# Where the 128 unread filling steps of a TensorE queue stand, and how wide their products are

## The chip, the cores and the metric

The kernel runs on one core of one Trainium2 chip. The metric is device time in microseconds (us) of one launch, from which the median over several runs is taken. A profiled execution has a time of its own, and inside it a span, from the first to the last instruction that the profiler shows.

## The reference

The computation has two stages. The first is a recurrent attention (RWKV7) over 768 time steps for 4 batches x 8 heads, with a 40x40 state for each of the 32 sequences. The second is a normalised SwiGLU feed-forward network on the 3072 x 320 result.

```python
for t in range(S):                                   # S = 768
    y[:, :, t] = einsum('bhd,bhde->bhe', rt, state)
    Sa = einsum('bhde,bhe->bhd', state, at)
    state = state * wt[:, :, None, :] - einsum('bhd,bhe->bhde', Sa, bt) + einsum('bhd,bhe->bhde', vt, kt)
...
xn = x / sqrt(mean(x * x) + 1e-6) * rms_g            # x: (3072, 320)
g, val = xn @ w_gate, xn @ w_val                     # (320, 1536) each
out = (g * sigmoid(g)) * val @ w_out                 # (1536, 320)
```

The feed-forward weights arrive in 64-bit floating point.

## The kernel before, in words

The 768 time steps are cut into 24 chunks of 32. For each chunk `front(c)` loads the chunk's inputs, turns them (TensorE transposes, line 479) and makes the chunk's triangular matrices level by level (`gramk`, line 476: the steps named A,K and Ab,K). `inverse(c)` sends the triangular matrix through DRAM into another layout (DMA sB, M), inverts it on VectorE (Yi and tmp) and sends it back (DMA sY, LT). `main(c)` solves for the chunk's update (the steps Xs,LT and Xs,LB, used in the first five chunks), updates the state (VU,KN and ST), and makes the chunk's output y (the steps As,KN and As,kbn, one for each level), which is normalised and turned into `xg`. `feed(g)` then runs the feed-forward network for one or two chunks: twelve column blocks with weights `wf`, accumulated into the PSUM tile `po` (line 476, po<-wf,hT). The weights are narrowed from 64 to 32 bits once, in pieces, by `narrow` (lines 988 to 996 and the helpers: tiles `wf`, `exs`, `o`, on VectorE and ScalarE, with loads from GpSimd's queue); this is laid among the first chunks.

No scheduler runs. Each operation is recorded as a `Piece` by `Plan.add`, in the order of the Python code, and `Plan.issue` issues the pieces in the order of the table `ORDER`, written out by hand. A number in `ORDER` counts from the first piece that is not yet issued; 0 is that piece itself. So numbers after a moved piece change even where the order of the other pieces doesn't. Each engine then works through its own queue in that order and waits in it where an input isn't there yet.

The intermediate results of TensorE live in three PSUM tiles, ps0 to ps2. Each use of one is a "room", and the table `PAIRS` says for each room which of the three it gets.

The last 128 pieces are recorded at the end of the kernel function (lines 1024 to 1029) and are of kind "idle". Each issues two bf16 products of 128x128 by 512 columns of the identity's bits into the half `po_[:, 1]` of `po`. Nothing reads what they write; the first product of the network's accumulation overwrites it. They wait for nothing but the identity, and no other engine waits for them. In this text such a piece is a filling step, and its two products are fillers. All of them stand in the first 166 us.

## Time and profile before

| | us |
|---|---|
| runs: median (lowest to highest, 3 runs) | 1004.35 (996.09 to 1010.13) |
| the profiled execution, its own time | 1002.48 |
| its span | 1000.7 |
| TensorE busy in the span | 955.2 |
| VectorE busy | 776.7 |
| ScalarE busy | 507.3 |
| GpSimd busy | 343.4 |
| fillers (line 1028), 256 products, busy | 70.5 |
| TensorE's mean granted clock | 0.994 |

In the profile PE is TensorE, PEld its weight loads, DVE VectorE, ACT ScalarE, POOL GpSimd and SP the queue engine; a q behind a name is the engine's sequencer. A float32 product of one matmul stands as two instructions in the trace, a transpose and a filler as one. The ends of matmuls are modelled, so that the time from start to start says more of their pace than their own length. The granted clock (PEclk in an answer by stretches) is the share of full speed at which TensorE was let run.

### The profile page before, as it was taken

Reading aid. Unit: us, or ns where it says so; the run is one execution under the profiler, and the core shown is the slowest. Engines: PE = TensorE matmul, PEld = TensorE weight load, DVE = VectorE, ACT = ScalarE, POOL = GpSimd, SP = SyncE. Lnnn points to the kernel's source line nnn. Section 1 sums busy time; section 2 is a strip of 40 time slices with the busy share of each in tenths; the row PEclk is TensorE's granted clock in tenths of the full one; section 3 lists DMA queues with packets and bytes.
Section 4 is the critical chain, followed back from the end, with each engine's and each line's share of the span. In section 5 each row is a group of like instructions: output and inputs, shape, how many; then the busy total and the mean of one; then the engine's idle time right before and its main releaser. Section 6 shows DMA issues by size and latency. Waiting matters only on the chain.

```text
span 1000.7 us, 55765 instructions
## 1 busy us (share of the span) xinstructions
PE 955.2 (95%) x24768; PEld 754.0 (75%) x24768; DVE 776.7 (78%) x2721; ACT 507.3 (51%) x1133; POOL 343.4 (34%) x592
## 2 busy tenths in 40 slices
PE   8788799999999999999999999999999899999998
PEld 4455557877877887888888788878787787788877
DVE  9998877786977977977969878879689588676541
ACT  6787467455454444454553554545544445435131
POOL 8887353231242333334132333331504224211000
PEclk9999999999999999999999999999999999999999
DMA  8665343322233323233132332332323232320100
GB/s 176 170 178 134 81 110 76 66 53 51 43 68 69 52 63 76 44 79 77 25 73 40 78 78 41 77 72 37 79 57 59 55 63 60 63 40 17 41 11 20
DMA packets 139025, 68.89 MB, mean 69 GB/s; under 512 B 119617, under 2 KB 126113, under 8 KB 138785
## 3 DMA queue, kind: packets, MB, share of 16 engines
q0 software_dynamic: 19680, 32.48, 15.5%
q1 hardware_dynamic: 116928, 32.53, 14.8%
q8 instruction: 194, 3.18, 1.3%
q10 hardware_dynamic: 2176, 0.33, 0.2%
q14 instruction: 47, 0.38, 0.1%
HBM read 55.05 MB, written 10.22 MB: 65 GB/s over the span
## 4 chain that ended last, share of the span: by engine, by line
PE 71%; DVE 11%; DMA 6%; ACT 4%; issue 4%; POOL 2%; SPq 2%; DVEq 0%; ACTq 0%; POOLq 0%
PE ps L476 51%; PE po L476 13%; PE ps L479 6%; DVE Yi L430 2%; SPq L473 2%; DMA M<-sB 2%; DMA sB<-LT 2%; DMA LT<-sY 1%; PE po L1028 1%; DVE tmp L430 1%; DVE LT L430 1%; DVE As L430 1%; ACT VU L457 1%; DMA sY<-Yi 1%; DVE K L430 1%
## 5 line engine op out<-in xcount | busy, mean ns | idle before, releaser
L476 PE MATMUL ps<-xg,wf 128*128 128x256 f32 (+3 forms) x1872 | 362.4, 375 | 2.6 <-DVE hT L430 2.5
L476 PEld LDWEIGHTS ps<-xg,wf 128*128 128x128 f32 (+1 forms) x1872 | 268.1, 189 | 51.4 <-issue 5.9
L476 PE MATMUL po<-wf,hT 128*128 128x320 f32 x576 | 178.5, 442 | 0.3 <-DVE hT L430 0.3
L476 PEld LDWEIGHTS po<-wf,hT 128*128 128x128 f32 x576 | 104.7, 190 | 34.4 <-DVE hT L430 0.5
L430 DVE TENSOR_TENSOR Yi<-Yi,tmp 128x24 f32<-128x24 f32 (+21 forms) x512 | 107.3, 210 | 11.0
L430 DVE TENSOR_TENSOR tmp<-Yi,M 128x24 f32<-128x24 f32 (+21 forms) x512 | 107.4, 210 | 10.9 <-DMA M<-sB 0.3
L430 DVE TENSOR_TENSOR hT<-ps,sg 128x256 f32<-128x256 f32 (+1 forms) x156 | 60.1, 400 | 71.0 <-PE ps L476 49.0
L453 ACT ACTIVATE sg<-ps 128x256 f32<-128x256 f32 (+1 forms) x156 | 55.0, 369 | 110.7 <-PE ps L476 110.2
L463 POOL TENSOR_TENSOR ss<-ss,mhalf 128x1 f32<-128x1 f32 x24 | 16.9, 704 | 252.2 <-DVE ss L430 237.7
L457 ACT COPY KN<-ps 128x640 f32<-128x640 f32 x95 | 65.7, 693 | 70.0 <-DVE LT L430 29.5
L430 DVE TENSOR_TENSOR K<-K,T 128x256 f32<-128x256 f32 (+1 forms) x191 | 93.7, 502 | 2.9 <-PE ps L476 1.7
L430 DVE SCALAR_TENSOR_TENSOR Yi<-M,Yi 128x27 f32<-128x27 f32 (+7 forms) x228 | 46.2, 243 | 52.6 <-DMA M<-sB 25.3
L473 POOL DMA_DIRECT2D kbn<-in_b_dram x92 | 53.9, 587 | 91.6 <-PE ps L476 90.6
L473 POOL DMA_DIRECT2D kbn<-in_k_dram x92 | 53.8, 587 | 81.7 <-PE ps L476 80.4
L476 PEld LDWEIGHTS ps<-Ab,K 64*60 64x60 f32 (+2 forms) x4608 | 66.1, 127 | 20.4 <-issue 9.0
L473 POOL DMA_DIRECT2D VU<-in_v_dram x92 | 54.0, 588 | 78.8 <-PE ps L476 74.9
L476 PE MATMUL ps<-Ab,K 64*60 64x56 f32 (+2 forms) x4608 | 73.0, 214 | 6.8 <-DVE K L430 2.6
L430 DVE TENSOR_TENSOR As<-ps,msi 128x256 f32<-128x256 f32 (+1 forms) x168 | 70.7, 455 | 7.6 <-ACT As L460 4.9
L476 PEld LDWEIGHTS ps<-As,KN 128*40 128x40 f32 x3072 | 63.9, 124 | 15.2 <-issue 5.5
L1028 PE MATMUL po<-ident 128*128 128x512 bf16 x256 | 70.5, 401 | 2.0 <-POOL ident L492 2.0
L476 PE MATMUL ps<-As,KN 128*40 128x32 f32 x3072 | 68.9, 204 | 3.4 <-ACT y L457 1.3
L457 ACT COPY K<-K 128x512 f32<-128x512 f32 x95 | 60.6, 638 | 19.4 <-DVE K L430 6.9
(141 smaller groups left out, 1554.1 us busy)
## 6 DMA issues: line engine op xcount, KB each, us to landing
M<-sB SPq DMA_DIRECT2D x24, 512.0 KB, 4.4
wan<-in_r_dram SPq DMA_DIRECT2D x24, 160.0 KB, 3.7
kbn<-in_b_dram POOLq DMA_DIRECT2D x92, 40.0 KB, 3.1
VU<-in_v_dram POOLq DMA_DIRECT2D x92, 40.0 KB, 2.6
wan<-in_w_dram POOLq DMA_DIRECT2D x46, 80.0 KB, 2.9
wan<-in_a_dram POOLq DMA_DIRECT2D x46, 80.0 KB, 2.6
kbn<-in_k_dram POOLq DMA_DIRECT2D x92, 40.0 KB, 2.7
wn<-in_w_dram POOLq DMA_DIRECT2D x92, 40.0 KB, 2.8
```

What stands on the lines that cost most here:

```text
L430: plan.add("DVE", time + more + each * size(o), 0.087, lambda at: [fn(at(o), *m(at))], [o], aps(*args))
L453: scalar(o, [a], lambda at: nc.scalar.activation(at(o), at(a), f, **kw), aps(acc), 0.1 if f in (AF.Square, AF.Relu) else 0.0)
L457: scalar(o, [a], lambda at: nc.scalar.copy(at(o), at(a)), extra=more)
L463: plan.add("POOL", 0.5, 0.06, lambda at: nc.gpsimd.tensor_tensor(o, a, b, op), [o], [a, b])
L473: plan.add(by, 0.6 if by == "POOL" else 0.45, 0.0, lambda at: queue.dma_start(out=o, in_=i), [o], [i], load=load, since=since)
L476: return o, lhsT, rhs, lambda at: nc.tensor.matmul(at(o), lhsT, rhs, start=start, stop=stop, skip_group_check=True), 4
L479: return o, i, ident, lambda at: nc.tensor.transpose(at(o), i, ident), 2
L1028: nc.tensor.matmul(po_[:, 1], ones[:, 0:P], ones[:, None, :].to_broadcast((P, 2, 2 * P)), start=True, stop=True, skip_group_check=True)
```

## The change

Two things change. Each filler has 384 columns in place of 512. And the 128 filling steps stand at other places: the order of all other pieces is the same, piece for piece, on all engines, and the number of filling steps is too. From the chunk-0 output's last transposes on (the step ps<-ident,y at 76.30 us in the trace of before), the table `PAIRS` also has ps1 and ps2 exchanged.

```diff
 ORDER = """
 76 84 83 86 75 71 2 3 4 5 6 7 0 35 47 0 17 54 64 0 0 51 0 35 0 55 0 0 67 68 60 187 188 41 49 368 59 71 369 0
-35 0 0 0 46 353 374 182 5903 5904 5905 5906 5907 73 0 32 167 168 178 75 74 73 0 1 27 3 0 362 2 0 346 367 337 170 2 164 163 336 72 80
+35 0 0 0 46 353 374 182 5903 5904 5905 5906 5907 5908 5909 5910 5911 73 0 32 167 168 178 75 74 73 0 1 27 3 0 362 2 0 346 367 337 170 2 164
...
 PAIRS = """
-012020012010102101021011100001020010220212110200010202110021221002100001122012021010121222112121201101021101101102221210
+012020012010102101011012200002020020110121220100020101220012112001200002211021012020212111221212102202012202202201112120
...
     for n in range(IDLE):
         plan.add("PE", 0.0, 0.0, lambda at: [
-            nc.tensor.matmul(po_[:, 1], ones[:, 0:P], ones[:, None, :].to_broadcast((P, 2, 2 * P)), start=True, stop=True, skip_group_check=True)
+            nc.tensor.matmul(po_[:, 1, 0:384], ones[:, 0:P], ones[:, None, 0:192].to_broadcast((P, 2, 192)), start=True, stop=True, skip_group_check=True)
             for k in range(2)], [], [ident], kind="idle", many=4)
```

How many filling steps stand in front of a TensorE step, for the steps where it changes most or where the prediction speaks of it (times are starts in the trace of before):

| step | at us | before | after |
|---|---|---|---|
| ps<-ident,wan (first transposes) | 6.42 | 5 | 9 |
| ps<-A,K (chunk 1) | 30.50 | 6 | 0 |
| ps<-ident,kbn (chunk 2) | 47.82 | 13 | 23 |
| ps<-ident,K (chunk 1) | 51.62 | 4 | 1 |
| ps<-Xs,LB (chunk 0) | 56.59 | 1 | 4 |
| ps<-rE,vut (chunk 0) | 64.10 | 1 | 0 |
| ps<-As,KN and As,kbn (chunk 0, four steps) | 68.99 to 72.15 | 3 | 0 |
| ps<-Xs,LT (chunk 1) | 77.21 | 1 | 0 |
| ps<-Ab,K (chunk 2, last) | 91.62 | 3 | 4 |
| ps<-As,kbn and VU,KN (chunk 1) | 99.36, 101.25 | 1, 1 | 0, 0 |
| ps<-ST,aP (chunk 2) | 109.91 | 1 | 0 |
| ps<-ident,K (chunk 2) | 113.27 | 3 | 0 |
| ps<-Xs,LT (chunk 2, first) | 124.31 | 1 | 7 |
| ps<-Xs,LB (chunk 2) | 126.85 | 4 | 1 |
| ps<-As,kbn (chunk 2) | 141.38 | 1 | 6 |
| ps<-As,KN (chunk 2, third and fourth) | 143.72, 145.90 | 1, 1 | 2, 0 |
| ps<-ident,wan; ident,x; Xs,LT | 148.78, 150.34, 152.80 | 5 | 0 |
| all steps from Xs,LT to ps<-xg,wf | 155.90 to 166.11 | 5 | 0 |

Three places on TensorE. The first is the output of chunk 1, at 98 to 101 us: the level steps with chunk 1's factors KN_1 and kbn_95, and the update VU_99. Before:

```order
L476 MATMUL ps_65<-As_136,KN_1_107 40x32 x16
L1028 LDWEIGHTS ident
L1028 MATMUL po<-ident 128x512
L1028 LDWEIGHTS ident
L1028 MATMUL po<-ident 128x512
L476 MATMUL ps_65<-As_136,kbn_95 40x32 x16
L476 MATMUL ps_63<-As_136,KN_1_113 40x32 x16
```

After, at the same place on TensorE:

```order
L476 MATMUL ps_64<-As_136,KN_1_107 40x32 x16
L476 MATMUL ps_64<-As_136,kbn_95 40x32 x16
L476 MATMUL ps_63<-As_136,KN_1_113 40x32 x16
L476 MATMUL ps_65<-VU_99,KN_1_115 40x40 x32
L476 MATMUL ps_63<-As_136,KN_1_111 40x32 x16
```

The filling step between the two level steps is gone, and so is the one ahead of VU_99; ps_64 and ps_65 (ps1 and ps2) are exchanged.

The second place is TensorE at 25 to 30 us, between chunk 0's VU_98,LT_102 (the first product of its solve) and chunk 1's first A_122,K_121. Before, where eleven more fillers follow the last row:

```order
L1028 LDWEIGHTS ident
L1028 MATMUL po<-ident 128x512
L476 MATMUL ps_65<-VU_98,LT_102 32x40 x32
L1028 LDWEIGHTS ident
L1028 MATMUL po<-ident 128x512
```

After, on TensorE from the transposes of kbn_95 on:

```order
L479 MATMUL ps_65<-ident,kbn_95 104x64 x16
L479 MATMUL ps_63<-ident,K_120 128x40 x16
L479 MATMUL ps_64<-ident,wan_93 104x64 x16
L476 MATMUL ps_65<-VU_98,LT_102 32x40 x32
L476 MATMUL ps_63<-A_122,K_121 64x56 x32
L476 MATMUL ps_64<-Ab_124,K_120 60x56 x32
```

Twelve filling steps that stood between these six rows are gone; the next filler comes behind the last row.

The third place is TensorE at 157 to 163 us, chunk 4's first level steps (A_122,K_120 and Ab,K) and the transposes of chunk 3's VU_99. Before:

```order
L1028 LDWEIGHTS ident
L1028 MATMUL po<-ident 128x512
L476 MATMUL ps_65<-A_122,K_120 64x56 x32
L479 MATMUL ps_64<-ident,VU_99 104x64 x16
L1028 LDWEIGHTS ident
L1028 MATMUL po<-ident 128x512
L1028 LDWEIGHTS ident
L1028 MATMUL po<-ident 128x512
L476 MATMUL ps_63<-Ab_123,K_121 60x56 x32
L476 MATMUL ps_64<-Ab_124,K_120 56x56 x32
```

After, on TensorE:

```order
L476 MATMUL ps_65<-Xs_133,LT_103 32x40 x32
L476 MATMUL ps_64<-A_122,K_120 64x56 x32
L479 MATMUL ps_65<-ident,VU_99 104x64 x16
L476 MATMUL ps_63<-Ab_123,K_121 60x56 x32
L476 MATMUL ps_65<-Ab_124,K_120 56x56 x32
```

No filling step stands here or later; before, the last one stood at 165.68 us.

## The prediction, made before the result was known

> **What bounds the kernel now.** I read the page first, then the fillers alone by stretch, then the chain of waits in the part that holds them, then TensorE in order of time.

> ```profile
> span 1000.7 us, 55765 instructions
> PE 71%; DVE 11%; DMA 6%; ACT 4%; issue 4%; POOL 2%; SPq 2%; DVEq 0%; ACTq 0%; POOLq 0%
> L1028 PE MATMUL po<-ident 128*128 128x512 bf16 x256 | 70.5, 401 | 2.0 <-POOL ident L492 2.0
> ```

> The chain that ended last is 71% TensorE. The fillers are one group of 256 products; the 2.0 us of idle time before them is the start. Now the fillers alone in three stretches (stretch, its length, busy time and count on PE and PEld, granted clock, DMA share, GB/s), and below them, for the first stretch, all engines (PE, PEld, DVE, ACT, POOL).

> ```profile
> 0.00:62.00 62.00, 31.82 (x118) 10.64 (x118) 0.97 0.74 179
> 62.00:170.00 108.00, 38.63 (x138) 10.01 (x138) 0.97 0.46 107
> 170.00:1000.70 830.70, 0.00 (x0) 0.00 (x0) 1.00 0.27 56
> ```

> ```profile
> 0.00:62.00 62.00, 49.35 (x1030) 26.75 (x1030) 57.82 (x187) 45.97 (x83) 52.40 (x103) 0.97 0.74 179
> ```

> After 170 us there is no filler, the clock is full, and nothing in the order changes: 831 us can only be moved as a whole. So the change is worth what it does before 170 us. In the first 62 us VectorE is busy for 57.82 us, with weight narrowing, and the chain has no piece of line 1028; a filler there costs nothing so far. From 62 us on the chain has these (start, length, what; 16 pieces, of which I quote the first, the last and those that the sum uses):

> ```profile
> 63.64 0.54 PE po L1028 x2
> 76.74 0.54 PE po L1028 x2
> 90.13 1.40 PE po L1028 x6
> 98.89 0.54 PE po L1028 x2
> 100.78 0.54 PE po L1028 x2
> 109.44 0.54 PE po L1028 x2
> 111.94 1.40 PE po L1028 x6
> 113.96 0.54 PE po L1028 x2
> 125.09 1.83 PE po L1028 x8
> 145.00 0.97 PE po L1028 x2
> 148.31 0.54 PE po L1028 x2
> 163.09 0.54 PE po L1028 x2
> 165.84 0.43 PE po L1028 x2
> ```

> The three pieces left out are like the one at 163.09 (two products, 0.54 us; at 155.43, 156.69 and 159.34). All sixteen make 12.0 us, the 1.2% that the chain's summary gives to this line. This is time in which a filler ran and the chain's next step stood behind it.

> **Pace of a filler.** TensorE in order of time (start, length, what, count, idle time before and what ended it):

> ```profile
> 2.04 4.45 PE L1028 MATMUL po<-ident 128*128 128x512 bf16 x10 [2.04 <-POOL ident L492]
> 25.57 0.79 PE L476 MATMUL ps<-VU,LT 32*32 32x40 f32 x64
> 30.50 1.16 PE L476 MATMUL ps<-A,K 64*64 64x56 f32 x64 [1.44 <-ACT KN L457]
> 39.39 5.79 PE L1028 MATMUL po<-ident 128*128 128x512 bf16 x26
> 47.82 1.10 PE L479 MATMUL ps<-ident,kbn 64*104 64x64 f32 x16 [2.64 <-POOL kbn L469]
> 56.59 0.79 PE L476 MATMUL ps<-Xs,LB 16*32 16x40 f32 x64 [0.85 <-ACT Xs L457]
> 83.41 1.81 PE L476 MATMUL ps<-A,K 64*64 64x56 f32 x64
> 141.38 0.81 PE L476 MATMUL ps<-As,kbn 128*40 128x32 f32 x32 [1.69 <-ACT x L460]
> 143.72 1.28 PE L476 MATMUL ps<-As,KN 128*40 128x32 f32 x32
> 164.49 1.36 PE L476 MATMUL ps<-xg,wf 64*128 64x128 f32 x12
> ```

> At full clock 26 fillers take 5.79 us, 0.22 each; at the start, before the clock is up, ten take 4.45 us, 0.45 each. By columns (384 of 512) that becomes 0.17 and 0.33, so a filling step of two takes 0.33 us, or 0.67 at the slow clock. All 256 then take 43 us in place of 57. That the pace follows the columns is an assumption, though the slow and the full clock's 2 to 1 speaks for it.

> **Part by part: what leaves the path.** At ten places of 0.54 us on the chain, at 145.00 (0.97) and at 165.84 (0.43) the changed order has no filling step before that step any more: 10 x 0.54 + 0.97 + 0.43 = 6.8 us. At 125.09 four steps become one. The step behind them needs Xs, which ScalarE writes:

> ```profile
> 125.23 0.41 ACT L457 COPY Xs<-ps 128x320 f32<-128x320 f32 x1
> 127.76 0.44 ACT L460 ACTIVATE Xs<-ps 128x320 f32<-128x320 f32 x1 [0.94 <-PE ps L476]
> ```

> It is there at 125.64, 0.55 us after the piece's start, and ScalarE later waits 0.94 us for that step; so of 1.83 us about 0.6 stays, and 1.2 goes. The pieces at 90.13, 111.94 and 113.96 (3.3 us) get four, no and one step. I count them at nothing: what follows them is an operand that VectorE finishes at about the time the filler ends, so the filler becomes a pause. The bounds are 0 and 3.3. Together 8.0 us, with VectorE late next at the first two places (63.64 and 76.74, where it works nearly without a break) and TensorE itself from 143 us on.

> **What is put in front of pauses.** Twenty-three steps before the step at 47.82 take 7.7 us where the run and the idle time were 8.4; six before 141.38 take 2.0, where one step and 1.69 us of idle time were 2.2: both end in time. Nine at the very start take 18 x 0.33 = 5.9 us while the clock is slow, against 4.45; the first transposes come some 0.7 us later, since the clock rises on the way. This lies in the first 62 us, under VectorE's narrowing: 0, at worst 0.7.

> **The exchange of ps1 and ps2** is complete from 76 us on: the same uses follow each other in each. At the seam, at 76.30 and 77.21, two steps take each other's former tile. I take nothing, with one filling step's length, 0.5 us, as the bound on either side.

> **The clock.** The granted clock is the term with the worst bounds. Stretches of 3.41 us, all engines as above; the column of 0.50 and 1.00 is the clock:

> ```profile
> 43.96:47.37 3.41, 1.22 (x6) 0.37 (x4) 3.41 (x8) 2.92 (x5) 3.21 (x8) 1.00 0.78 175
> 47.37:50.78 3.41, 2.96 (x21) 1.63 (x22) 3.41 (x7) 3.41 (x7) 3.28 (x6) 0.50 0.78 232
> 78.09:81.50 3.41, 2.15 (x85) 1.07 (x87) 3.41 (x9) 1.09 (x3) 3.35 (x6) 1.00 0.69 188
> 81.50:84.92 3.42, 3.42 (x122) 2.49 (x117) 0.90 (x4) 2.65 (x7) 3.42 (x6) 0.50 0.69 215
> 122.46:125.87 3.41, 1.56 (x69) 1.09 (x69) 3.31 (x8) 3.38 (x7) 0.57 (x1) 1.00 0.30 45
> 125.87:129.29 3.42, 3.42 (x150) 2.18 (x149) 2.45 (x5) 2.48 (x6) 0.00 (x0) 1.00 0.52 170
> 139.53:142.94 3.41, 1.72 (x66) 1.42 (x66) 1.64 (x5) 2.03 (x5) 2.44 (x4) 1.00 0.64 96
> 142.94:146.36 3.42, 3.30 (x50) 1.74 (x50) 3.32 (x9) 0.69 (x2) 2.73 (x5) 0.50 0.51 112
> ```

> Three times the clock is halved for exactly one such stretch, each time after one in which TensorE did little. Its busy time doesn't tell which: 1.56 us at 122.46 is followed by full clock (the row of 125.87), 2.15 us at 78.09 is not. What does is an estimate of mine: each product counted by the share of the 128x128 array that it fills, times its columns, twice for float32, against the 8,000 columns that fillers at 0.22 us would stream in 3.41 us. In the stretch from 139.53 one filler (512) and 64 level products of 128x40 with 32 columns (64 x 2 x 32 x 40/128 = 1280) make 0.22. The two others before a halving come to 0.25 and 0.22, that at 122.46 to 0.29; the least among the rest is 0.31. So the limit would lie between 0.25 and 0.29, and a filler of 384 columns weighs 0.047 in place of 0.063.

> Price of a halved stretch on the path: the step A,K takes 1.81 us at 83.41 and 1.16 at 30.50 (+0.65), the level step 1.28 at 143.72 and 0.81 at 141.38 (+0.47). Two such steps: 1.1 us; at most half of 3.41, 1.7. Fillers in it double too.

> Gone should be the halvings at 47.37 (off the path) and 142.94, worth 0.6 beyond the filler at 145.00. That at 81.50 stays likely. New ones: with no filler between 25.57 and 33 us TensorE does nothing from 26.36 to 30.50, and between 49 and 54 us two steps stand where seven stood. Taking the fillers out of my estimate in place gives 0.21 at 98.6, 0.21 at 108.8 and 0.22 at 149.8, where the path runs through TensorE. I take these three at 1.1 each, 3.3 us. Work that moves together weighs more per stretch, which is why not more. In front of 56.59 four steps would take 2.7 us at the slow clock, where one step and 0.85 us of idle time were 1.4: up to 1.3 late for the solve, of which 1.0 may reach the step at 63.64.

> Sum: 8.0 + 0.6 - 3.3 - 1.0 = 4.3 us saved. Against the profiled execution's 1002.48 that is 998.2; against the median of 1004.35, 1.9 above it, 1000.0. I predict 999.

> [...]

> **Rivals.** *Starved array, slower.* Each filler taken from a busy place and each quarter cut from a product lowers the array's load, and 32 stretches lie between 62 and 170 us. If ten more than before are halved on the path, 10 x 1.1 + 1.0 is 4 us over the 8.0 that go: 1006.5. It decides from seven on. For it: six of my estimated loads lie near the limit, and a run of filling steps at half clock outlasts its pause. Against: three halvings with wider fillers, and the denser work. Chance 0.22.

> *Nothing moves.* Before 143 us the chain passes through VectorE, DMA and GpSimd's issues between the fillers, and what TensorE has earlier waits there. Only the pieces from 145.00 on count (0.97, 0.43 and five of 0.54: 4.1), less one or two halvings and the solve: 1002. Chance 0.25. A filler paced by something other than its columns would end here too.

> *All of it.* The pauses are filled, the clock is halved only off the path: 8.0 + 0.6 + 1.1 for the stretch at 81.50, which may go too, 9.7 us: 993. Chance 0.12.

> The forecast, 995.5 to 1001.5 in these terms, has 0.41.

> **Range and chances.** The cases reach from 993 to 1006.5; the bounds (3.3 at kept pieces, 1.7 a halving) add some 2 us at each end, and the three runs lie 14 us apart, so that a median may sit 3 or 4 us off. For 8 in 10: 990 to 1008. A measurement of this kernel tells about 2%, 20 us, from no change. Faster by that would need more than all 12.0 us of chain and all three halvings (5.1): 0.03. Slower by that would need some twenty halvings on the path: 0.03. Within: 0.94. Below the median of before at all: about 0.7.

> **What would show it.** Right: the first step after the fillers, ps<-xg,wf, at 164.49 now, starts 3 to 6 us earlier, and the rest is shifted by as much; line 1028 has under 4 us on the chain; fillers take 0.16 to 0.17 us each at full clock; more stretches at half clock than three, among them ones near 30 and 52 us. Wrong: fewer than three (all of it), over ten (starved), or the step at 164.49 where it was while the ones near 100 us came earlier (nothing moves).

## The result, and the profile after

The changed kernel takes 1013.91 us in the median of 20 runs (1007.93 to 1023.09); before took 1006.35 us in 20 runs on the same chips (996.09 to 1014.48). The ratio is 1.0078, with a 95 % interval of 1.0052 to 1.0104: 5 to 10 us slower, less than 2 %. The prediction of 999 us (990 to 1008) missed it, and in sign: 4.3 us saved were forecast, some 8 us were lost. Ratios and intervals in this document are of fast executions alone (one of the early layout with 14 steps, below, took 3392.58 us and is left out).

The profiled execution of the changed kernel took 1011.24 us (before: 1002.48). The chain's shares by line in before, and then the lines of the changed kernel's page that answer to those of before, with the same shares:

```profile
PE ps L476 51%; PE po L476 13%; PE ps L479 6%; DVE Yi L430 2%; SPq L473 2%; DMA M<-sB 2%; DMA sB<-LT 2%; DMA LT<-sY 1%; PE po L1028 1%; DVE tmp L430 1%; DVE LT L430 1%; DVE As L430 1%; ACT VU L457 1%; DMA sY<-Yi 1%; DVE K L430 1%
```

```profile
span 1009.5 us, 55764 instructions
PE 70%; DVE 12%; DMA 6%; ACT 5%; issue 4%; SPq 2%; ACTq 0%; DVEq 0%
PE ps L476 50%; PE po L476 13%; PE ps L479 6%; DVE Yi L430 3%; PE po L1028 2%; DVE tmp L430 2%; DMA M<-sB 2%; DMA sB<-LT 2%; SPq L473 2%; DVE LT L430 1%; DVE y L430 1%; DMA LT<-sY 1%; DVE As L430 1%; ACT VU L457 1%; DVE K L430 1%
```

Line 1028, the fillers, has 2 % of the chain where it had 1 %: 19.3 us by the sum of its pieces (17.0 of them between 62 and 172 us) in place of 12.0. It should have fallen to under 4 us. Its three stretches, all engines first (PE, PEld, DVE, ACT, POOL, then the granted clock), then the fillers alone (PE, PEld, clock):

```profile
0.00:62.00 62.00, 46.96 (x1026) 30.61 (x1026) 55.87 (x179) 43.62 (x78) 50.06 (x100) 0.86 0.73 174
62.00:170.00 108.00, 89.02 (x3118) 67.25 (x3117) 88.66 (x265) 72.58 (x153) 66.99 (x107) 0.86 0.46 108
170.00:1009.50 839.50, 818.86 (x20628) 669.75 (x20627) 631.75 (x2279) 390.79 (x904) 227.45 (x385) 0.99 0.27 55
```

```profile
0.00:62.00 62.00, 27.79 (x130) 13.17 (x130) 0.86 0.73 174
62.00:170.00 108.00, 28.26 (x128) 11.34 (x126) 0.86 0.46 108
```

The fillers are busy for 56 us in place of 70.5, as their width says. But the granted clock is 0.86 in both of the first stretches, where it was 0.97: 14 stretches of 3.41 us up to 170 us run at half clock, where 3 did. Five of them stand in a row (all engines, with the stretch before them and the one behind):

```profile
127.11:130.53 3.42, 2.36 (x112) 1.65 (x107) 3.38 (x6) 3.42 (x8) 0.57 (x1) 1.00 0.51 147
130.53:133.94 3.41, 3.11 (x73) 2.44 (x73) 1.61 (x9) 2.74 (x6) 1.64 (x3) 0.50 0.31 87
133.94:137.35 3.41, 2.51 (x81) 2.05 (x80) 2.96 (x15) 2.24 (x4) 3.41 (x7) 0.50 0.53 138
137.35:140.77 3.42, 3.19 (x74) 2.39 (x74) 1.00 (x4) 2.17 (x6) 3.31 (x6) 0.50 0.65 150
140.77:144.18 3.41, 3.28 (x108) 2.88 (x106) 3.19 (x13) 2.77 (x7) 1.78 (x3) 0.50 0.20 37
144.18:147.59 3.41, 3.41 (x12) 1.51 (x10) 1.76 (x4) 0.89 (x3) 0.83 (x2) 0.50 0.47 79
147.59:151.01 3.42, 3.32 (x114) 2.54 (x114) 1.37 (x4) 0.68 (x2) 2.12 (x4) 1.00 0.63 132
```

TensorE is busy for 2.5 to 3.4 us of each of the five, and stays at half clock all the same. TensorE in order of time, at the places of the sum (start, length, what, count, idle time before and what ended it):

```profile
32.03 1.97 PE L476 MATMUL ps<-A,K 64*64 64x56 f32 x64 [3.90 <-ACT KN L457]
...
40.93 7.65 PE L1028 MATMUL po<-ident 128*128 128x384 bf16 x46
...
56.92 2.40 PE L1028 MATMUL po<-ident 128*128 128x384 bf16 x8
59.26 0.79 PE L476 MATMUL ps<-Xs,LB 16*32 16x40 f32 x64
...
143.93 3.91 PE L1028 MATMUL po<-ident 128*128 128x384 bf16 x12
147.77 0.80 PE L476 MATMUL ps<-As,kbn 128*40 128x32 f32 x32
...
169.10 2.25 PE L476 MATMUL ps<-xg,wf 64*128 64x128 f32 x20
```

Since the order of everything but the fillers is the same, each step of TensorE has its counterpart in the trace of before, and the difference of the two starts is how late it is. (Steps are named by their start in the trace of before.) A,K of 30.50 starts at 32.03, 1.5 us late. The solve of 56.59 is 2.7 late, after eight fillers of 2.40 us. At 131.62 the delay is 2.5. As,kbn of 141.38 starts at 147.77, 6.4 late: its input was there at 143.66, but six filling steps stood ahead of it and took 3.91 us at half clock. The first step behind the fillers, ps<-xg,wf of 164.49, is 4.6 late where 3 to 6 early was forecast, and the step at 167.5 is 5.2 late. The other 3.5 us come behind 170 us, where nothing in the order changed.

### The profile page after: what moved, and what is told of

The parts are those of the page before. It is cut to its first block, busy times and chain, and to the rows that moved or that the text cites. A ratio compares the mean times of both kernels' runs of the same rounds, so it can differ in the third digit from the quotient of the medians.

```text
span 1009.5 us, 55764 instructions
## 1 busy us (share of the span) xinstructions
PE 954.8 (95%) x24768; PEld 767.6 (76%) x24768; DVE 776.3 (77%) x2721; ACT 507.0 (50%) x1133; POOL 344.5 (34%) x592
## 3 DMA queue, kind: packets, MB, share of 16 engines
q8 instruction: 194, 3.18, 1.3%
## 4 chain that ended last, share of the span: by engine, by line
PE 70%; DVE 12%; DMA 6%; ACT 5%; issue 4%; SPq 2%; ACTq 0%; DVEq 0%
PE ps L476 50%; PE po L476 13%; PE ps L479 6%; DVE Yi L430 3%; PE po L1028 2%; DVE tmp L430 2%; DMA M<-sB 2%; DMA sB<-LT 2%; SPq L473 2%; DVE LT L430 1%; DVE y L430 1%; DMA LT<-sY 1%; DVE As L430 1%; ACT VU L457 1%; DVE K L430 1%
## 5 line engine op out<-in xcount | busy, mean ns | idle before, releaser
L476 PE MATMUL ps<-xg,wf 128*128 128x256 f32 (+3 forms) x1872 | 364.7, 377 | 1.0 <-ACT sg L453 0.8
L476 PEld LDWEIGHTS ps<-xg,wf 128*128 128x128 f32 (+1 forms) x1872 | 269.4, 190 | 50.1 <-issue 5.5
L476 PE MATMUL po<-wf,hT 128*128 128x320 f32 x576 | 178.5, 442 | 0.2 <-DVE hT L430 0.2
L476 PEld LDWEIGHTS po<-wf,hT 128*128 128x128 f32 x576 | 104.8, 190 | 34.3 <-DVE hT L430 0.4
L457 ACT COPY KN<-ps 128x640 f32<-128x640 f32 x95 | 65.7, 693 | 73.2 <-DVE LT L430 30.9
L476 PEld LDWEIGHTS ps<-Ab,K 64*60 64x60 f32 (+2 forms) x4608 | 67.4, 129 | 17.9 <-issue 7.8
L476 PE MATMUL ps<-Ab,K 64*60 64x56 f32 (+2 forms) x4608 | 74.2, 216 | 6.1 <-issue 2.9
L476 PEld LDWEIGHTS ps<-As,KN 128*40 128x40 f32 x3072 | 63.4, 123 | 12.1 <-issue 5.2
L476 PE MATMUL ps<-As,KN 128*40 128x32 f32 x3072 | 68.1, 204 | 2.6 <-ACT As L460 0.7
L457 ACT COPY K<-K 128x512 f32<-128x512 f32 x95 | 60.4, 636 | 19.2 <-DVE K L430 6.3
L473 POOL DMA_DIRECT2D wn<-in_w_dram x92 | 52.5, 573 | 40.5 <-DVE KN L430 40.2
```

The lines of the kernel that those rows point to most:

```text
L457: scalar(o, [a], lambda at: nc.scalar.copy(at(o), at(a)), extra=more)
L473: plan.add(by, 0.6 if by == "POOL" else 0.45, 0.0, lambda at: queue.dma_start(out=o, in_=i), [o], [i], load=load, since=since)
L476: return o, lhsT, rhs, lambda at: nc.tensor.matmul(at(o), lhsT, rhs, start=start, stop=stop, skip_group_check=True), 4
```

## The experiments

The theory at the outset is the first rival: a **starved array**, with halved stretches that last, and filling runs that take twice as long there. Against it stood the width alone, the start alone, and chance behind 170 us. The layouts are given as filling steps in front of a step, before and in the experiment. Ratios are to before on the same chip. Where traces are compared, each is one execution.

**Width and layout apart.** First the width alone:

```diff
-nc.tensor.matmul(po_[:, 1], ones[:, 0:P], ones[:, None, :].to_broadcast((P, 2, 2 * P)), ...)
+nc.tensor.matmul(po_[:, 1, 0:384], ones[:, 0:P], ones[:, None, 0:192].to_broadcast((P, 2, 192)), ...)
```

> The order and the number of filling steps of before, only each product 384 columns wide. Starved array: each filler weighs 0.047 in place of 0.063 of a stretch, so some stretches near the limit of 0.25 fall under it; with the fillers still among the work I expect five to eight halved stretches before 170 us (3 before, 14 in the changed kernel), and a time of 1005 to 1010 us, less than half of the 7.6 us that the whole change cost. If the width alone is the cause, 1012 to 1016 and ten halvings or more. If the width is only shorter fillers on the chain (12.0 us x 1/4 = 3 us saved), 1003.

Then the changed order with the old width (the changed kernel with that line undone):

> The order of the changed kernel, each product 512 columns as before. Starved array: the places from which fillers were taken still fall under the limit (near 30, 52, 131 to 147 us), but a filling run weighs a third more than with 384; seven to twelve halvings before 170 us, 1008 to 1012 us. If only the width did the harm, the kernel is 2 to 5 us faster than before (1001 to 1004), with three to five halvings, since 8.0 us of filler leave the chain. If the slow filling runs in front of pauses are the price, it is slower than the changed kernel, 1015 and more, since the same runs are a third longer.

The width alone gives 1.0015 (0.9985 to 1.0045), with seven halved stretches before 170 us, as the starved array had it; it costs nothing that can be measured. The layout alone gives 1.0086 (1.0051 to 1.0121), the same as the whole change, with five halved stretches before 170 us where seven to twelve were expected. So the layout is the cause. But between 62 and 170 us its clock is at 0.99:

```profile
0.00:62.00 62.00, 49.37 (x889) 27.82 (x890) 54.78 (x174) 41.85 (x74) 48.04 (x99) 0.89 0.69 168
62.00:170.00 108.00, 86.75 (x3147) 59.52 (x3146) 89.07 (x266) 73.91 (x153) 65.94 (x109) 0.99 0.48 112
```

With the wider products none is halved from 65.0 to 170.8 us, and still the kernel is as slow. The halved clock alone is not the answer. In its trace 7.0 of the 8.2 us that the step at 167.5 is late are there at the solve of 56.59 already (2.7 of 5.2 in the changed kernel): with wide products the early part weighs most.

**Early and late part apart.** The counts of the changed kernel up to the step at 62.91 us and those of before behind it, and the other way round, both with 384 columns. (From here on kbn2 is the step ps<-ident,kbn of chunk 2, at 47.82.)

```diff
 filling steps in front of     before   changed   early   late
 the steps up to 62.91             59        68      68     59
 the steps behind                  69        60      69     60
 all                              128       128     137    119
```

> 384 columns; up to the step at 62.91 us the counts of the changed kernel, behind it those of before. The profile of the changed kernel has its step at 62.91 2.3 us late, and the one at 167.5 5.2 us late. If the start decides (nine steps ahead of the first transposes, 23 ahead of kbn2, four ahead of the solve), the step at 62.91 is 2 to 2.5 us late again, and the kernel is 1010 to 1013 us. Starved array later: the delay at 62.91 shrinks behind it where the chain waits for DMA and VectorE, and the kernel is at 1006 to 1009, with no series of halvings from 130 us on.

> 384 columns; up to the step at 62.91 us the counts of before, behind it those of the changed kernel. Starved array: the series of five halved stretches from 130.5 to 147.6 us is there again, and the step at 141.38 waits some 4 us behind six filling steps at half clock; the step at 167.5 is 3 to 5 us late, 1009 to 1012 us. If the start decides, the step at 62.91 is where it was and the kernel is at 1004 to 1007.

Both come out above the whole change: 1.0112 (1.0077 to 1.0147), whose interval reaches into that of the change, and 1.0237 (1.0198 to 1.0276), clear of it. Neither theory had that. The second has its step at 167.5 where before has it (-0.07 us), and loses its time far behind all fillers. What TensorE waited for behind 170 us (what, us in total, times, longest), before and then this kernel, whose lines are numbered one lower:

```profile
PE ps L476 <- issue: 4.2, 6, 1.2
```

```profile
PE ps L475 <- issue: 24.4, 27, 3.3
```

These are pauses in which the engine waited for nothing that the profile shows, in the middle of a run of equal products. The longest, in order of time:

```profile
407.45 0.41 PE L475 MATMUL ps<-Xs,LT 32*32 32x40 f32 x22
411.14 1.00 PE L475 MATMUL ps<-Xs,LT 32*32 32x40 f32 x42 [3.28 <-issue]
```

The solve's 64 product instructions are cut behind the 22nd. A queue of the page's list of transfers (packets, MB, share), the same in every trace here (but for one packet more where 128 instructions were added, below), gives a lead:

```profile
q8 instruction: 194, 3.18, 1.3%
```

3.18 MB in 194 packets are 16 KB each; shared among TensorE's 49,536 products and weight loads they are 64 bytes for one, so a packet holds 256 instructions of TensorE. Numbering all of TensorE's instructions in the trace (in before 49,797, with 261 that are neither product nor load), this pause stands ahead of number 20673 = 80 x 256 + 193, and a packet had landed 1.44 us before its end. The two kernels here differ from before in the number of TensorE's instructions, by +36 and -36 (nine steps of two products with a load each), so every later packet begins at another place in the work. That made a new theory, of **instruction packets**: a stretch of work in which 256 instructions go by faster than the next packet lands ends in a pause, and where the boundaries fall depends on how many instructions went before. From the trace of before alone (the times at which TensorE passes each 256 instructions, and the landing times of its packets) I worked out what the pauses would become with other shifts. Three tests followed, with small products as mere instructions.

```diff
+    SMALL = {47: 64}
     for n in range(IDLE):
...
-            for k in range(2)], [], [ident], kind="idle", many=4)
+            nc.tensor.matmul(po_[0:32, 1, 0:8], ones[0:32, 0:32], ones[0:32, None, 0:4].to_broadcast((32, 2, 4)), start=True, stop=True, skip_group_check=True)
+            for k in range(SMALL[n])] if n in SMALL else [
...
+            for k in range(2)], [], [ident], kind="idle", many=4)
```

Step 47 is one more step, in front of the step at 47.82 in before. The second test has 18 small products there (36 instructions) and the late layout, the third the early layout with fewer steps:

```diff
 filling steps in front of               before   second test      third test
 the steps up to 62.91 but for kbn2      46      as before (46)   as changed (45)
 kbn2                47.82               13      13 + 18 small    14
 the steps behind                        69      as changed (60)  as before (69)
```

> Before, with 64 products of 8 columns more (128 instructions of TensorE, loads counted) in the pause ahead of kbn2 at 47.82 us, which has 2.64 us to spare. Theory of the instruction packets: in the traces so far TensorE gets its instructions in packets of 16 KB (256 instructions), and its long unexplained pauses stand at instruction numbers 193 above a multiple of 256, 1.2 to 1.6 us after such a packet has landed. 128 instructions more shift every later boundary by half a packet. Worked out from the chunk lengths and landing times in the trace of before, the pauses behind 170 us would grow by some 35 us, so 1030 to 1045 us, with the step at 62.91 us at most 1 us late. Starved array: nothing changes behind 62 us, 1005 to 1009.

> The kernel with the early counts of before and the late counts of the changed kernel (1032.7 us, 2.4 % slower than before), with 18 products of 8 columns more (36 instructions) ahead of kbn2: the number of TensorE's instructions up to 170 us is that of before again. Instruction packets: the pauses behind 170 us fall from 22 us to the 4 to 10 us of before, and the kernel comes back to 1006 to 1012 us although work was added. If the late layout itself cost the 2.4 % (starved array, order), it stays at 1028 or above.

> The kernel with the early counts of the changed kernel and the late ones of before (1.1 % slower), with 14 in place of 23 filling steps ahead of kbn2, so that the instruction numbers behind 48 us are those of before. Instruction packets: 1009 to 1014 if the start alone (nine steps at the start, none at 30.5 us, four ahead of the solve) costs 2 to 4 us; its pauses behind 170 us are back at 4 to 10 us from 14.8. If the start costs nothing, 1005 to 1008; if the start is the whole cost, it stays at 1018 and more.

Before with 64 small products more takes 1.0427 (1.0377 to 1.0477) of its time, 43 us more. They lie in the pause ahead of kbn2, and that step is on time:

```profile
45.21 1.75 PE L1029 MATMUL po<-ident 32*32 32x8 bf16 x64
47.92 0.66 PE L479 MATMUL ps<-ident,kbn 64*104 64x64 f32 x16 [0.96 <-POOL kbn L469]
```

Its pauses behind 170 us, in the same view as above:

```profile
PE ps L476 <- issue: 39.2, 34, 3.6
```

35 us more than the 4.2 of before, and 35 were worked out. Of the other 8 us, 4.0 are there at the step at 167.5 (1.4 at 62.91, where at most 1 was expected); the rest is not followed here. The late layout with 18 small products added is back at 1.0003 (0.9973 to 1.0033), from 1.0237: work was added and 23 us went. Its row:

```profile
PE ps L476 <- issue: 7.9, 10, 2.3
```

The early layout with nine steps fewer ahead of kbn2 comes to 1.0039 (1.0004 to 1.0073), from 1.0112. Over all eighteen traces there are 169 pauses of this kind (no cause shown) of 0.35 us or more behind 170 us. All stand at an instruction number of exactly 193 above a multiple of 256, and each ends 1.18 to 1.65 us after a packet landed. The theory holds: the packets' size (16 KB, at 64 bytes for one instruction) and the spacing of the pauses (whole multiples of 256 instructions) agree.

The changed kernel has 128 filling steps as before, so behind 166 us its boundaries are those of before, and its pauses there are no worse (6.5 us and, in a second trace, 5.4 in the same view, against 4.2 and up to 10.2 in the others with 128 steps). The packets explain the two hybrid kernels, but the loss of the change itself only where the numbers differ, before 166 us. There the changed kernel does have more of them. Its waits without a cause between 62 and 172 us:

```profile
PE ps L476 <- issue: 4.7, 5, 2.3
PE po L1028 <- issue: 2.8, 2, 1.5
PE ps L479 <- issue: 1.1, 1, 1.1
```

That is 8.6 us, all of it at number 193 above a multiple of 256, and 8.5 in its second trace, where the two traces of before have 3.6 (all at 193 too) and 4.5. The 2.8 us stand ahead of a filler and need not be on the path, and no run tells this part of the loss from the rest.

The second test says something of the change too. From 62.91 us on it has the layout and the instruction numbers of the changed kernel, and it takes 1.0003 (0.9973 to 1.0033) where the changed kernel takes 1.0078 (1.0052 to 1.0104). So the late part by itself costs nothing that can be measured; the loss needs the changed start, alone or together with the late part.

**A second trace of both.** The changed kernel and before once more:

> The changed kernel once more, for a second trace. What belongs to the change (shifts up to 170 us) should be there again: the step at 62.91 some 2 us late, the one at 167.5 4 to 6 us late, with a series of halved stretches between 130 and 148 us. What is chance should not: the halvings at 246 and 489 us.

> Before once more, for a second trace. If the profiled 1002.48 us of before was a lucky execution, the second lies near the median of the runs shown, 1006 to 1011, with one to four halved stretches behind 170 us and 8 to 14 us of pauses at packet boundaries. Instruction packets: the pauses stand at the same instruction numbers.

The changed kernel took 1015.39 us. A,K of 30.50 is 2.3 us late, the step at 131.62 7.5, that at 141.38 11.5 and the one at 167.5 10.6, with 16 halved stretches before 170 us and the same series of five from 135.7 on. So the growth between 131.62 and 141.38 is there again (4.0 us; 3.9 in the first trace), and the halvings at 246 and 489 us are not. Before took 1005.74, with its step at 167.5 0.8 us early and its end 3.3 us late against the first trace. Up to 170 us before repeats within about 1 us; behind it two executions lie 4 us apart. The 3.5 us of the changed kernel there are of that size, and I don't ascribe them.

**The late part, with the small products later.** The late layout again, with the 18 small products at 212 us in place of 47 us, with 384 and with 512 columns. The instruction numbers are those of before up to 62 us and behind 212 us, and differ from them by up to 36 in between:

```diff
-    SMALL = {47: 18}
+    SMALL = {119: 18}
```

> The kernel with the early counts of before and the late ones of the changed kernel, 384 columns (1032.7 us), with the 18 products of 8 columns (36 instructions) in the pause ahead of the score step at 212.44 us, in place of ahead of kbn2. Up to there its instruction numbers are those of the kernel that had its step at 167.5 us where before has it (-0.07); behind it they are those of before. Instruction packets: no series of pauses behind 212 us (4 to 10 us in place of 22), 1003 to 1008 us. If the late layout with its starved stretches costs time by itself, 1010 or more; if its 8.0 us of fillers off the chain were a gain that the pauses hid, 998 to 1001.

> The same with products of 512 columns. The changed layout with 512 columns had no halved stretch at all between 62 and 170 us. Starved array: wider products keep the clock up between 130 and 150 us, so that the step at 141.38 is not behind six slow filling steps, and the kernel is 1 to 3 us faster than the one with 384 (1001 to 1006). Filler off the chain: faster than before by up to 8 us (998). Instruction packets alone: as with 384 columns, 1003 to 1008.

They give 1.0030 (0.9992 to 1.0069) and 1.0036 (1.0003 to 1.0070). The forecast gain of 8 us isn't there in any width. What TensorE waited for between 62 and 172 us in the first of them, and in before:

```profile
PE ps L476 <- issue: 8.0, 7, 3.1
PE ps L479 <- DVE y L430: 3.6, 3, 1.7
```

```profile
PE ps L476 <- issue: 3.6, 5, 1.1
PE ps L479 <- DVE y L430: 1.1, 2, 0.6
```

Of the fillers that left, some came back as pauses without a shown cause, like those at packet boundaries, 4.4 us more, and some as waits for VectorE, 2.5 us more. The chain between 62 and 117 us shows it too, in before and in the late layout without small products (all in the summary by line):

```profile
by line: PE ps L476 22.2%; issue 13.9%; PE po L1028 11.0%; DVE As L430 9.1%; DMA wan<-in_a_dram 8.3%; DMA sY<-Yi 7.2%; DVE y L430 6.3%; DVE wf L996 4.5%; PE ps L479 4.4%; DVE LT L430 4.0%; DVE wf L430 3.6%; DVE tmp L430 2.7%; DVE Yi L430 2.
```

```profile
by line: issue 13.0%; DVE y L429 9.7%; POOL wf L472 9.0%; DVE As L429 6.5%; PE ps L475 5.9%; DMA kbn<-in_b_dram 5.5%; DVE tmp L429 5.0%; DVE wf L429 4.6%; POOL ss L462 4.5%; POOL wn L472 4.3%; DMA wf<-in_moe_w_gate_dram 4.1%; DVE Yi L429 4.
```

The fillers have left this stretch of the chain altogether, and between 62 and 172 us they have 3.9 us on it where they had 12.0 (the sum of the pieces of their line). TensorE's own steps fell from 22.2 % to 5.9 %, GpSimd and VectorE took their place, and the step behind the fillers begins at 163.88, 0.6 us earlier than before. That fits fillers that stood beside a chain of VectorE and GpSimd that was about as long. The shares are of one execution each, though: the second trace of before, without any edit, has 11.1 % where the first has 22.2 %.

**The early part.** Three places around the solve alone, and then the two halves of that, all with 384 columns on the layout of before and with kbn2's run taking up the difference:

```diff
 filling steps in front of          before   solve   four   two
 kbn2                47.82              13      15     10    18
 K                   51.62               4       1      4     1
 Xs,LT               53.64               3       1      3     1
 Xs,LB (the solve)   56.59               1       4      4     1
```

> The counts of before, 384 columns, but for three places: one filling step in place of four and of three ahead of the two steps at 51.62 and 53.64, and four in place of one ahead of the solve at 56.59, with two more ahead of kbn2 to keep the instruction numbers. In the traces with the changed start the solve begins 0.9 to 4.4 us later against before than the step in front of it. If the four steps at half clock are the price of the early part, the step at 62.91 is 1.5 to 3 us late and the kernel is at 1008 to 1010 us; if the start (nine steps ahead of the first transposes and no filler ahead of 30.5 us) is, the step at 62.91 is at most 0.7 us late, and the kernel is within 2 us of before.

> The counts of before, 384 columns, with four filling steps in place of one ahead of the solve at 56.59, and three fewer ahead of kbn2. The steps ahead of 51.62 and 53.64 keep their four and three. If the four steps are the price, the solve begins 1.3 to 3.3 us late, as with the whole edit (+3.30), also where the clock is full: eight products at 0.17 us are 1.4 us against 0.4 and 0.85 of pause, so some 0.1 late at full clock, 1.3 at half. If the starved stretch ahead is the price, the clock is not halved for more than one stretch between 47 and 57 us, the solve is at most 0.5 us late, and the kernel is within 2 us of before.

> The counts of before, 384 columns, with one filling step in place of four and of three ahead of the steps at 51.62 and 53.64, and five more ahead of kbn2; one step ahead of the solve as before. If the starved stretch is the price by itself, two or three stretches from 50 us on are halved, and the solves and turns that follow to 62.91 run at half clock, 1 to 2 us late there, 1007 to 1009 us. If the four steps are the price, the halving is there but hidden by the pauses, and the step at 62.91 is at most 0.7 us late.

In the traces the whole edit has the solve 3.3 us late and the step at 167.5 5.9 late; the four steps alone 4.9 and 6.1; the missing five alone 1.6 and 0.5. TensorE at the solve, with four steps, and with one:

```profile
58.86 2.74 PE L1028 MATMUL po<-ident 128*128 128x384 bf16 x8
61.53 1.29 PE L476 MATMUL ps<-Xs,LB 16*32 16x40 f32 x64
```

```profile
57.47 0.82 PE L1028 MATMUL po<-ident 128*128 128x384 bf16 x2
58.22 1.29 PE L476 MATMUL ps<-Xs,LB 16*32 16x40 f32 x64
```

Both run at half clock there (in the second for five stretches on end), so the halving by itself hardly reaches the step at 167.5 (at 62.91 it does, with 1.6 us), and the long run in front of a chain step does. The times don't tell them apart: 1.0032 (0.9995 to 1.0069), 1.0019 (0.9984 to 1.0053) and 1.0024 (0.9988 to 1.0059). The order of the prices is thus read from one trace each.

**Undone within the changed kernel.** The three places around the solve as before, with two steps fewer ahead of kbn2; and one step ahead of 141.38 in place of six, with five moved to the steps at 126.85, 128.11 and 129.96 (the expectation gives them a little early):

```diff
 filling steps in front of          changed   first   second
 kbn2                 47.82              23      21       23
 K                    51.62               1       4        1
 Xs,LT                53.64               1       3        1
 Xs,LB (the solve)    56.59               4       1        4
 126.85, 128.11, 129.96               1,0,0   1,0,0    4,1,1
 As,kbn              141.38               6       6        1
```

> The changed kernel with the counts of before at the three places around the solve (four, three, one), and two fewer ahead of kbn2. If that edit is the price of the early part, the kernel is 3 to 4 us faster than the changed one: 1.003 to 1.005 of before in place of 1.008, and the solve is no later against before than the step ahead of it. If the start (nine steps and none at 30.5) carries it, it stays at 1.007 to 1.009.

> The changed kernel with one filling step ahead of the step at 141.38 in place of six; the five others stand ahead of three steps at 125.8 to 129 us, where before had them. Starved array with slow filling runs: the loss between 131.6 and 141.4 us (3.9 and 4.0 us in the two traces of the changed kernel) falls to at most 1 us, and the kernel comes to 1.003 to 1.006 of before. If the delay there comes from the packets and the halved products alone, the loss stays at 3 us or more and the kernel at 1.008.

The first comes to 1.0040 (1.0006 to 1.0074), the second to 1.0050 (1.0013 to 1.0086), both as the theory had it, though the intervals reach into that of the whole change. In the trace of the first the loss ahead of the solve has not gone (it grows by 1.2 us from 47.82 to 56.59, as in the changed kernel by 1.1), so this run doesn't show the solve as the price within the change. The second does show its place. TensorE there, the run of 12 now a run of two:

```profile
144.31 0.82 PE L1028 MATMUL po<-ident 128*128 128x384 bf16 x2
145.24 1.28 PE L476 MATMUL ps<-As,kbn 128*40 128x32 f32 x32
```

From 131.62 to 141.38 the delay shrinks by 0.2 us where it grew by 3.9 and 4.0, although this stretch is still at half clock from 141.1 on. The series from 130.5 us is gone.

All eighteen traces bear this place out. The step's input is ScalarE's last write to x. With one filling step ahead (ten traces) the step of 141.38 starts within 0.4 us of it. With six it starts 0.6 to 1.5 us behind it in the four traces in which the run is at full clock, 2.8 and 3.4 in two in which part of it is at half clock, and 4.1 and 4.2 in the two of the changed kernel. But the delay at 167.5 is still 4.5 us in this last experiment, where the changed kernel had 5.2, since its trace is 4.0 late at 131.62 already; and 1.0050 and 1.0078 don't tell the two kernels apart.

No kernel here is faster than before.

## Why the prediction was wrong

**The step that failed** is the sum's first term: "Together 8.0 us, with VectorE late next at the first two places". The fillers did leave the chain in the two traces of the late layout in which the run ahead of 141.38 wasn't slowed: 12.0 us became 3.9 and 6.4. (In the changed kernel they have 17.0 and 17.5.) But the steps behind them came no sooner: in these two traces the step at 167.5 is at -0.07 and +0.56 us of before, where 8.0 were to be gained. By the waits above, VectorE and the instruction packets were late next, and not at two places alone; place by place this was not followed. The second trace of before says the same without any edit: there the fillers have 5.3 us of the chain in place of 12.0, and the step at 164.49 is 0.8 us earlier. A share of the chain was taken for a saving. For this term the rival "nothing moves" was right, and did not go far enough: it kept 4.1 us for the places from 145.00 on, where the changed kernel gained 1.2 and 0.9 us from 141.38 to 167.5.

**"This lies in the first 62 us, under VectorE's narrowing: 0, at worst 0.7"** failed too. In the seven traces with the changed start and with either width, A,K of 30.50 is 1.0 to 2.8 us late; in the ten others it is within 0.25 us of before. The chain of that one trace showed no filler, but a first run of 18 fillers at the start was near enough to it: the first transposes are 0.1 to 2.0 us late in the seven, and A,K waits for KN from ScalarE. At the start the fillers follow each other at 0.43 us in the trace of before and at 0.32 in that of the changed kernel, and from 7.01 and 8.40 us on at 0.22 and 0.16; the first entry of the granted clock, at full, begins at 6.41 and 7.65 us. (The clock in an answer by stretches counts as full where there is no entry.) A,K then runs at half clock (1.97 us in place of 1.16) and adds to it. What carries how much was not tried apart. At 62.91 the seven are 2.3 to 7.5 us late.

**"Both end in time"** was right for the run ahead of 47.82 where the clock was full (46 fillers in 7.65 us, 7.7 forecast; kbn2 was the last to wait for) and wrong for the six steps ahead of 141.38. I priced them at full clock, 2.0 us; they took 3.91 at half, and the step came 4.1 us after its input was there. Even at full clock it came 0.6 to 1.5 us after it. This is the largest single delay in the first trace of the change; that it makes the time longer no run shows. Doubling was in the working for the four steps ahead of 56.59 ("up to 1.3 late"), and these were indeed 1.4 us late (59.26 against an input ready at 57.91). The rule that served there should have been put to every run that was moved in front of a step on the path.

**The clock** was mis-sized: three new halvings on the path were taken, 3.3 us. Between 62 and 170 us nine stretches were halved in place of two, and the three that were named (98.6, 108.8 and 149.8) were not among them. The estimate of the array's load was right in kind for this trace: the stretches before a halving came to 0.00 to 0.26, with one exception (0.31 at 113.46), those that stayed at full clock at 0.25 to 0.31 and up. Over all traces it is rougher: by the same count, stretches of some 0.2 to 0.35 stand on both sides. What it left out is that at half clock fewer columns go by in 3.41 us (a filler of 384 takes 0.33 us there in place of 0.166): loads of 0.20 to 0.27 went with five halved stretches on end, up to one with 11 fillers (load 0.52), behind which the clock was full. With the wider products of the second experiment none was halved from 65.0 to 170.8 us, but in the late layout with 18 small products at 212 us five were with either width. So what the quarter that was cut does to the clock stays open; to the time it hardly matters. Idle time alone didn't tell the halvings: TensorE was busy for 2.36 us of the 3.42 from 127.11 on, ahead of the series, and for 2.5 to 3.4 us of each stretch in it, and the pause ahead of A,K (3.90 us from 28.13 on) began only at the instant at which the clock was halved. What sets the clock was not shown.

**Right** were the pace of a filler (0.166 and 0.33 us measured, 0.17 and 0.33 forecast), the exchange of ps1 and ps2 (the late layouts carry it, with the step at 167.5 at -0.07 us in one), halvings near 30 and 52 us (at 28.13 and 52.02), and that the first step behind the fillers tells it: over ten halvings were named as the mark of the starved array, and there were 14 and 16. That rival, at 1006.5, had the sign and the mechanism of the largest delay, with too small a price: it kept the 8.0 us. **Not in the working** at all were the pauses at the instruction packets (6.5 us behind 170 us in the changed kernel), which are a part of the "issue" of 4 % in the chain.

The traces' account of the change up to 170 us, for the first of them: 1.5 us from the start, 1.0 by 131.62, 3.9 in the series at half clock, -1.2 behind it, 5.2 in all. For the second: 2.3, 5.2, 4.0, -0.9, 10.6; of its 5.2 the most (6.0) is a wait for kbn ahead of 47.82 from GpSimd's side that no other trace has: one GpSimd copy (msi<-msk, 64x16) takes 6.49 us there, from 46.89 on, and 0.25 to 0.44 in the seventeen others. Why it took so long stays open. The sum of the early and the late part run apart, 0.4 and 0.0 to 0.3 %, is less than the whole 0.8 %, within the intervals. So the layout is shown as the cause, and the start as a part that it needs; how the loss divides among the start, the run ahead of 141.38 and the packets' pauses before 166 us stays open.

## What to carry to other kernels

What a step has on the chain of waits was no measure here of what its removal saves (fillers of 12.0 us on it became 3.9, and the step at 167.5 came 0.07 us earlier): look at how long the other engines' work beside it is, and take a second trace, before a share of the chain goes into a sum. Price every run of filling work that is put in front of a step of the path at half clock, since it is put there because the engine has little to do, and that is where the clock was low here (six steps took 3.91 us in place of 2.0). And keep the number of TensorE's instructions ahead of a tuned stretch, or reckon where its packets of 256 will begin: 128 instructions that fitted into a pause cost 43 us here.

## What the runs showed of the hardware

Half clock can last: it went on for five stretches (17.1 us) with TensorE busy for 2.5 to 3.4 of 3.41 us in each. That the low load of the slowed array keeps it there would fit these figures, and was not tested.
